# Last MLP as an explicit pipeline with residuals on the tensor engine, score repeats counted ahead of each slot, and a norm's root in four pieces

## The chip, the cores and the metric

The kernel runs on one core of one Trainium2 chip. The metric is the device time of one execution in microseconds (us); medians over several executions are quoted. A "span" is the time from the first to the last instruction of the one execution that was profiled; it is about 2 us shorter than the device time of that execution. The engines: **PE** (TensorE, matmuls), **PEld** (its weight loads), **ACT** (ScalarE, here the exponentials), **DVE** (VectorE), **SP** (SyncE, which only issues transfers here). DVE takes its instructions in the order of the program, so one that waits holds back those behind it: below, DVE stands 7.36 us before one reciprocal, and the copy listed after it runs only then.

## The reference

Two transformer layers on 2048 rows of 512 columns, 32 heads of 16, an MLP of width 1792, all bfloat16; A and B use the same weights in both layers.

```python
x = A_x                                              # (1, 2048, 512)
x = x + A(layernorm(x), A_wqkv, A_wo)                # 32 heads, softmax(q k^T / 4) v, then @ wo
x = x + B(layernorm(x), B_w1, B_w2)                  # relu(x @ w1) @ w2
x = x + A(layernorm(x), A_wqkv, A_wo)                # second layer
return x + B(layernorm(x), B_w1, B_w2)
```

## The kernel before

The loop runs over "slots" of three score blocks (128 keys by 512 queries of one head each). In a slot PE makes scores (32-row tiles), ACT takes their exponential, PE multiplies the exponentials with the values (32-column tiles). Some blocks' exponentials are made on DVE, in chains of several steps; two such blocks are a "pair", and each pair takes work off ACT. All other work (projections, MLP, norms) is kept in queues and fitted into gaps. Three places matter.

**1. Repeated score matmuls.** PE repeats a slot's scores to stay busy; the aim is that its clock isn't lowered:

```python
MM = 216.0                      # ns of one matmul step
FLOOR = 0.56                    # share of a slot in which PE should be busy
...
spare = int(max(need_by - pe_start("s", s_ready), 0.0) / MM)
times = 1 + min(spare, 0 if level >= 0 else 1 if level > -MM else 2)
for _ in range(times):
    ...                         # three score matmuls, the same result each time
...
level = min(level + busy[0] - FLOOR * (exp_end[no] - exp_end[no - 1]), 90.0)
```

**2. The sums of a "segment"** (four heads, 512 queries). `u` holds the unnormalised outputs and the rows of sums. The sums go to 128 partitions in a small transfer (c<-u), are inverted, go back (u<-c) and are broadcast (r<-u, 256 KB); then one DVE multiply makes `ot`. There are two buffers of each, so segment n waits for the multiply of segment n - 2:

```python
if n > 1:
    run_until(("m", n - 2))
u, r, c = ubuf[n % 2], rbuf[n % 2], cbuf[n % 2]
...
nc.sync.dma_start(out=c[:], in_=sums); mark(("c", n), lag=2600.0)   # planner: there after 2.6 us
...
def recip():
    nc.vector.reciprocal(out=c[:], in_=c[:])
    nc.sync.dma_start(out=sums, in_=c[:])
    nc.sync.dma_start(out=r[:], in_=...)            # broadcast of each row to 32 partitions
    mark(("r", n), lag=8500.0)
...
if last:
    task(5000, direct, ots, [("po",)])              # last segment: shuffle, no transfer
else:
    task(250, recip, [("r", n)], [("c", n)])        # at the end of DVE's queue
    task(700, lambda: mul(0, QS), ots + [("m", n)], [("r", n)] + war)
```

`run_until` emits the task at once, whatever it must wait for.

**3. The tail.** After the last slot, `run_all()` emits what is left in the queues, one group of matmuls after the other: output projection, DVE adds x, norm, transposes, all 14 groups of the MLP's first matrix, then the second's.

The softmax here doesn't subtract the row's maximum and nothing guards it: scores larger than these inputs give would overflow.

## Time and profile before

| | before |
|---|---|
| median (4 runs) | 1855.53 us (1851.55 to 1857.51) |
| span of the profiled execution | 1860.6 us |
| end of ACT's last exponential | 1788.4 us |
| tail, from there to the end | 72.2 us |
| ACT idle ahead of exponentials | 28.9 us |

Three more lines of before: the first two are from the groups of instructions (busy us, mean ns of one, idle time of the engine just before them and what ended it); the third is a row of the table of stretches, with the columns that the prediction explains.

```profile
L903 PE MATMUL ps_s<-q,ktp 32*128 32x512 bf16 x6099 | 706.5, 394 | 145.6 <-ACT e L926 127.6 <-DVE ktp L462 1.7 <-DVE x L515 0.6
L664 DVE RECIPROCAL c<-c 128x16 f32<-128x16 f32 x63 | 15.5, 246 | 36.8 <-DMA c<-u 36.8
...
1120.00:1140.00 20.00, 16.00 (x106) 3.42 (x104) 4.26 (x8) 16.07 (x12) 0.00 (x0) 0.67 0.16 33
```

DVE stood for 36.8 us before reciprocals, waiting for the small transfer of the sums. Between 1120 and 1140 us ACT lost 3.93 us at a clock of 0.67.

### The profile page before, as it was taken

To read this page: it belongs to the slowest core of one execution; us is meant where nothing else is said; L and a number is where in the kernel's file an instruction comes from. 1 tells how busy PE (TensorE), PEld (TensorE's weight loads), DVE (VectorE), ACT (ScalarE), POOL (GpSimd) and SP (SyncE) were. 2 spreads that over 40 slices of the span, in tenths; PEclk is the share of its full clock that TensorE was granted. 3 is DMA by queue.
4 is the path that set the end of the run, shared out by engine and by line. 5 is a ranking of instruction groups with operands and counts; after the bars stand their busy time and mean duration, and the time that the engine had idled before them with its cause. 6 is when DMAs were issued, how large, how long until landed. Compare 5 with 4: busy or idle time off the path is not lost.

```text
span 1860.6 us, 28967 instructions
## 1 busy us (share of the span) xinstructions
PE 1660.1 (89%) x12509; PEld 521.9 (28%) x12509; DVE 1170.9 (63%) x1796; ACT 1749.7 (94%) x1380; POOL 2.4 (0%) x35
## 2 busy tenths in 40 slices
PE   8898889999889999899999889989988999889966
PEld 2222222322222232223232221222222222222222
DVE  7446767777766975778332224776767767586662
ACT  6999998999999999999999998999999999999940
POOL 0000000000000000000000000000000000000000
PEclk9999998999999999999899986999999999999988
DMA  4000000210001000110010001011000110001001
GB/s 142 1 13 8 19 13 7 44 22 12 8 21 44 9 11 13 36 25 12 13 29 12 1 19 25 13 33 30 18 16 13 36 30 19 13 19 41 21 9 39
DMA packets 92739, 42.20 MB, mean 23 GB/s; under 512 B 76612, under 2 KB 84548, under 8 KB 92612
## 3 DMA queue, kind: packets, MB, share of 16 engines
q1 hardware_dynamic: 91268, 39.06, 9.3%
q8 instruction: 97, 1.59, 0.4%
q10 hardware_dynamic: 1344, 1.31, 0.2%
q14 instruction: 30, 0.25, 0.0%
HBM read 20.71 MB, written 2.10 MB: 12 GB/s over the span
## 4 chain that ended last, share of the span: by engine, by line
ACT 84%; PE 10%; DVE 3%; DMA 2%; issue 0%; SPq 0%; DVEq 0%
ACT e L926 84%; PE ps_s L903 4%; PE ps_o L696 2%; PE ps_s L360 2%; PE ps_f L360 1%; DMA c<-u 1%; DVE stats L379 0%; DMA r<-u 0%; DMA wqkv<-in_A_wqkv_dram 0%; DVE ht L542 0%; DVE q L497 0%; DVE vaug L490 0%; DVE ot L656 0%; DVE r L678 0%; DMA u<-c 0%
## 5 line engine op out<-in xcount | busy, mean ns | idle before, releaser
L926 ACT ACTIVATE e<-ps_s 128x1536 bf16<-128x1536 f32 (+1 forms) x1366 | 1741.2, 1588 | 28.9 <-PE ps_s L903 27.9
L903 PE MATMUL ps_s<-q,ktp 32*128 32x512 bf16 x6099 | 706.5, 394 | 145.6 <-ACT e L926 127.6
L696 PE MATMUL ps_o<-e,vaug 128*32 128x512 bf16 x3862 | 554.0, 399 | 6.7 <-DVE u L643 3.3
L903 PEld LDWEIGHTS <-ktp 32*128 32x128 bf16 x6099 | 216.7, 93 | 577.6 <-issue 521.2
L696 PEld LDWEIGHTS <-vaug 128*32 128x32 bf16 x4564 | 163.7, 94 | 461.3 <-issue 435.1
L737 DVE TENSOR_SCALAR di<-ps_s 128x512 int32<-128x512 f32 x234 | 160.8, 688 | 101.2 <-PE ps_s L903 99.8
L767 DVE SCALAR_TENSOR_TENSOR de<-dy,di 128x1024 bf16<-128x1024 f32 x117 | 143.1, 1223 | 8.9 <-PE ps_o L696 2.5
L767 DVE SCALAR_TENSOR_TENSOR dy<-dm 128x1024 f32<-128x1024 f32 x117 | 142.9, 1221 | 2.4
L767 DVE SCALAR_TENSOR_TENSOR dy<-dy,dm 128x1024 f32<-128x1024 f32 x117 | 142.8, 1220 | 2.1
L542 DVE TENSOR_SCALAR ht<-ps_f 128x512 bf16<-128x512 f32 x99 | 68.1, 688 | 101.3 <-PE ps_f L360 100.8
L360 PE MATMUL ps_f<-xn2T,w 128*128 128x512 bf16 x400 | 122.5, 383 | 3.4 <-DVE ht L542 0.6
L360 PE MATMUL ps_f<-w,ht 128*128 128x512 bf16 x392 | 123.3, 385 | 0.5
L656 DVE SCALAR_TENSOR_TENSOR ot<-u,mask,r 128x512 bf16<-128x512 f32 (+1 forms) x67 | 48.0, 716 | 82.1 <-DMA r<-u 82.0
L360 PE MATMUL ps_f<-xnT,wqkv 128*128 128x512 bf16 x280 | 88.8, 392 | 4.2 <-DVE vaug L490 1.4
L497 DVE TENSOR_SCALAR q<-ps_f,qmask 128x512 bf16<-128x512 f32 x78 | 55.9, 744 | 48.2 <-PE ps_f L360 48.1
L696 PE MATMUL ps_o<-de,vaug 128*32 128x512 bf16 x468 | 84.2, 387 | 0.0
L761 DVE TENSOR_SCALAR di<-di 128x1024 int32<-128x1024 int32 x117 | 80.8, 691 | 2.9
L761 DVE TENSOR_SCALAR dm<-di 128x1024 int32<-128x1024 int32 x117 | 80.6, 689 | 1.5
L360 PE MATMUL ps_f<-wo,ot 128*128 128x512 bf16 x224 | 71.6, 389 | 0.9 <-DVE x L515 0.4
L696 PE MATMUL ps_o<-di,vaug 128*32 128x512 bf16 x234 | 58.8, 395 | 0.0
L360 PEld LDWEIGHTS <-w 128*128 128x128 bf16 x448 | 36.2, 98 | 73.4 <-issue 59.3
L360 PEld LDWEIGHTS <-ht 128*128 128x128 bf16 x448 | 34.5, 97 | 70.1 <-issue 57.0
(74 smaller groups left out, 496.2 us busy)
## 6 DMA issues: line engine op xcount, KB each, us to landing
r<-u SPq DMA_DIRECT2D x63, 256.0 KB
w<-in_B_w_dram SPq DMA_DIRECT2D x112, 128.0 KB
out_dram<-x SPq DMA_DIRECT2D x16, 128.0 KB
x<-in_A_x_dram SPq DMA_DIRECT2D x14, 128.0 KB
w<-in_B_w_dram SPq DMA_DIRECT2D x1, 1792.0 KB
wqkv<-in_A_wqkv_dram ACTq DMA_DIRECT2D x2, 512.0 KB
c<-u SPq DMA_DIRECT2D x63, 8.0 KB
u<-c SPq DMA_DIRECT2D x63, 8.0 KB
```

Of the source, the lines that this page charges most:

```text
L360: nc.tensor.matmul(b, lhsT, rhs, start=(i == 0), stop=(i == n - 1))
L497: nc.vector.tensor_scalar(out=qbuf[n % 2][e][:], in0=b, scalar1=qmask[e][:, 0:1], scalar2=None, op0=ALU.mult,)
L542: nc.vector.tensor_scalar(out=ht[ft], in0=b, scalar1=0.0, scalar2=None, op0=ALU.max)
L656: nc.vector.scalar_tensor_tensor(out=ot[t][:, a : a + w], in0=u[:, a : a + w], scalar=mask[e][:, 0:1], in1=r[:, a : a + w], op0=ALU.mult, ...
L696: nc.tensor.matmul(ps_o[32 * g : 32 * g + 32, :], vaug[sg["l"]][kb][:, 4 * sg["T"] + g, 2 * e : 2 * e + 32], rhs, start=g not in sg["begun ...
L737: first = nc.vector.tensor_scalar(out=di[:, half, :].bitcast(I32), in0=src, scalar1=EXP_BIAS, scalar2=0.0, op0=ALU.add, op1=ALU.max,)
L761: nc.vector.tensor_scalar(out=out[:].bitcast(I32), in0=di[:].bitcast(I32), scalar1=keep, scalar2=put, op0=ALU.bitwise_and, op1=ALU.bitwise_or,
L767: nc.vector.scalar_tensor_tensor(out=out[:], in0=x[:], scalar=c, in1=y[:], op0=ALU.add, op1=ALU.mult)
L903: nc.tensor.matmul(b[:, w, :], kt[32 * g : 32 * g + 32, kc : kc + P], qbuf[sg["n"] % 2][sg["e"]][32 * g : 32 * g + 32, :], start=True, sto ...
L926: ex = nc.scalar.activation(out=eb[:, :m, :], in_=b[:, :m, :], func=ACTF.Exp, scale=1.0 / (LOG2E * UNIT),)
```

## The change

Its intent: (a) keep PE's clock up by counting the repeats that a slot will need before it runs, instead of paying back a debt one slot late; (b) write out the tail by hand, with h and z matmuls alternating, the residual opened in PSUM by an identity matmul, and copies shared by ACT and DVE; (c) let other DVE work in between the pieces of a norm's root; (d) shorten the start.

```diff
-        times = 1 + min(spare, 0 if level >= 0 else 1 if level > -MM else 2)
+        short = FLOOR * 1330.0 - level - busy[0] - MM * (1 + (len(pend) > 1))
+        times = 1 + min(spare, max(0, math.ceil(short / MM)))
...
-            task(2400, lambda: ln_rstd(tag), [("rs", tag)], all4("st", tag))
+            for part in range(4):
+                task(600, lambda part=part: ln_rstd(tag, part), [("rs", tag, part)], ...)
...
-            task(5000, direct, ots, [("po",)])
+            last_steps.append(direct)
         else:
-            task(250, recip, [("r", n)], [("c", n)])
+            task(250, recip, [("r", n)], [("c", n)], place=0)
...
     run_all()
+    free, lasts = ps_s[1 - slot[0] % 2], ps_s[slot[0] % 2]
+    banks = [free[:, w, :] for w in range(W)] + [ps_f[:]]
+    more = [lasts[:, w, :] for w in range(W)] + [ps_o[:]]
+    for i in rows:
+        add(banks[i], ident[:], x_t[j * TPC + i][:], True, False)      # residual
+        for t in range(NT - 1):
+            add(banks[i], ot[t][:, i * P : (i + 1) * P], wo[:, t // 2, :], False, False)
+    for i in rows:
+        last_steps[0](i)
+        add(banks[i], ot[NT - 1][...], wo[...], False, True)
+        nc.scalar.copy(out=x_t[j * TPC + i][:], in_=banks[i])
+    ...                                             # statistics, root, scales, transposes
+    for ft in range(NF + 1):                        # h(ft), relu on DVE or ACT, then z(ft - 1)
+        ...
```

In this excerpt two assignments are joined into one line and long argument lists are cut ("..."). At the start, the masks go ahead of the first norm and all four scales ahead of the transposes.

More of the change, by code (lines that the diff above doesn't have):

```diff
@@ L380, in ln_stats, with ln_rstd @@
         nc.vector.bn_aggr(out=mv[ln_n(tag)][:, i, :], in_=st[:])
-    def ln_rstd(tag):
+    def ln_rstd(tag, part):
         n = ln_n(tag)
         a, y, t1 = va_[n], ya_[n], ta_[n]
-        nc.vector.tensor_scalar(
-            out=a[:], in0=mv[n][:, :, 1], scalar1=EPS, scalar2=None, op0=ALU.add
-        )
-        nc.vector.tensor_scalar(
-            out=t1[:].bitcast(I32), in0=a[:].bitcast(I32), scalar1=1, scalar2=None,
-            op0=ALU.logical_shift_right,
-        )
-        nc.vector.tensor_scalar(
-            out=y[:].bitcast(I32), in0=t1[:].bitcast(I32), scalar1=-1.0,
-            scalar2=float(RSQRT_SEED), op0=ALU.mult, op1=ALU.add,
-        )
-        for _ in range(3):
-            nc.vector.scalar_tensor_tensor(
-                out=t1[:], in0=y[:], scalar=-0.5, in1=y[:], op0=ALU.mult, op1=ALU.mult
-            )
-            nc.vector.tensor_mul(out=t1[:], in0=t1[:], in1=a[:])
-            nc.vector.scalar_tensor_tensor(
-                out=y[:], in0=t1[:], scalar=1.5, in1=y[:], op0=ALU.add, op1=ALU.mult
-            )
+        if part == 0:
+            nc.vector.tensor_scalar(
+                out=a[:], in0=mv[n][:, :, 1], scalar1=EPS, scalar2=None, op0=ALU.add
+            )
+            nc.vector.tensor_scalar(
+                out=t1[:].bitcast(I32), in0=a[:].bitcast(I32), scalar1=1, scalar2=None,
+                op0=ALU.logical_shift_right,
+            )
+            nc.vector.tensor_scalar(
+                out=y[:].bitcast(I32), in0=t1[:].bitcast(I32), scalar1=-1.0,
+                scalar2=float(RSQRT_SEED), op0=ALU.mult, op1=ALU.add,
+            )
+            return
+        nc.vector.scalar_tensor_tensor(
+            out=t1[:], in0=y[:], scalar=-0.5, in1=y[:], op0=ALU.mult, op1=ALU.mult
+        )
+        nc.vector.tensor_mul(out=t1[:], in0=t1[:], in1=a[:])
+        nc.vector.scalar_tensor_tensor(
+            out=y[:], in0=t1[:], scalar=1.5, in1=y[:], op0=ALU.add, op1=ALU.mult
+        )
     def ln_apply(tag, j, i):
@@ L411, in ln_apply, with ln_transpose @@
         )
-    def ln_transpose(tag, i):
-        pt = bank().bitcast(BF16)
+    def ln_transpose(tag, i, b=None):
+        pt = (bank() if b is None else b).bitcast(BF16)
         for c in range(NDC):
@@ L429, in ln_rows @@
         if i == TPC - 1:
-            task(2400, lambda: ln_rstd(tag), [("rs", tag)], all4("st", tag))
+            for part in range(4):
+                task(
+                    600, lambda part=part: ln_rstd(tag, part), [("rs", tag, part)],
+                    [("rs", tag, part - 1)] if part else all4("st", tag),
+                )
             for k in range(TPC):
@@ L433, in ln_rows @@
                     420, lambda k=k: ln_apply(tag, j, k), [("xn", tag, k)],
-                    [("xT", prev, k), ("rs", tag)],
+                    [("xT", prev, k), ("rs", tag, 3)],
                 )
@@ L538, in fin @@
         def fin(b):
-            if wide[0] and ft % 2:
-                nc.scalar.activation(out=ht[ft], in_=b, func=ACTF.Relu)
-            else:
-                nc.vector.tensor_scalar(
-                    out=ht[ft], in0=b, scalar1=0.0, scalar2=None, op0=ALU.max
-                )
+            nc.vector.tensor_scalar(
+                out=ht[ft], in0=b, scalar1=0.0, scalar2=None, op0=ALU.max
+            )
             mark(("h", l, j, ft))
@@ L623 @@
     norm_no = [0]
+    last_steps = []
     def finish_segment(sg, last):
@@ L673, in recip, with direct @@
             mark(("r", n), lag=8500.0)
-        def direct():
-            nc.vector.stream_shuffle(out=r[:], in_=u[:], mask=[lane] * 32)
-            for a in range(0, QS, P):
-                nc.vector.reciprocal(out=r[:, a : a + P], in_=r[:, a : a + P])
-                mul(a, P)
+        def direct(i):
+            if i == 0:
+                nc.vector.stream_shuffle(out=r[:], in_=u[:], mask=[lane] * 32)
+            a = i * P
+            nc.vector.reciprocal(out=r[:, a : a + P], in_=r[:, a : a + P])
+            mul(a, P)
         ots = [("ot", l, j, t, i) for i in range(TPC)]
         if last:
-            task(5000, direct, ots, [("po",)])
+            last_steps.append(direct)
         else:
-            task(250, recip, [("r", n)], [("c", n)])
+            task(250, recip, [("r", n)], [("c", n)], place=0)
             task(700, lambda: mul(0, QS), ots + [("m", n)], [("r", n)] + war)
-        if t == NT - 1:
+        if t == NT - 1 and not last:
             work.extend(rest_of_chunk(l, j))
@@ L802 @@
     idle_matmuls(18)
-    for i in range(TPC):
-        ln_stats(tag, 0, i)
-    ln_rstd(tag)
-    for i in range(TPC):
-        ln_apply(tag, 0, i)
-        pt = ln_transpose(tag, i)
-        if i % 2:
-            nc.vector.tensor_copy(out=xnT[0][:, :, i * P : (i + 1) * P], in_=pt)
-        else:
-            nc.scalar.copy(out=xnT[0][:, :, i * P : (i + 1) * P], in_=pt)
-        mark(("xnT", tag, i))
-        idle_matmuls(1)
     for e in range(2):
@@ L824 @@
         )
+    for i in range(TPC):
+        ln_stats(tag, 0, i)
+    for part in range(4):
+        ln_rstd(tag, part)
+    for i in range(TPC):
+        ln_apply(tag, 0, i)
+    for i in range(TPC):
+        pt = ln_transpose(tag, i)
+        if i % 2:
+            nc.scalar.copy(out=xnT[0][:, :, i * P : (i + 1) * P], in_=pt)
+        else:
+            nc.vector.tensor_copy(out=xnT[0][:, :, i * P : (i + 1) * P], in_=pt)
+        mark(("xnT", tag, i))
+        idle_matmuls(1)
     for i in range(3):
@@ L965, with add @@
         run_dve(0.0, musts)
-    wide[0] = True
     run_all()
+    l, j = 1, NQS - 1
+    tag = ("ln2", l, j)
+    rows = range(TPC)
+    free = ps_s[1 - slot[0] % 2]
+    lasts = ps_s[slot[0] % 2]
+    banks = [free[:, w, :] for w in range(W)] + [ps_f[:]]
+    more = [lasts[:, w, :] for w in range(W)] + [ps_o[:]]
+    def add(b, lhsT, rhs, first, last):
+        nc.tensor.matmul(b, lhsT, rhs, start=first, stop=last)
+    for i in rows:
+        add(banks[i], ident[:], x_t[j * TPC + i][:], True, False)
+        for t in range(NT - 1):
+            add(banks[i], ot[t][:, i * P : (i + 1) * P], wo[:, t // 2, :], False, False)
@@ new lines @@
+    for i in rows:
+        x = x_t[j * TPC + i]
+        last_steps[0](i)
+        add(banks[i], ot[NT - 1][:, i * P : (i + 1) * P], wo[:, (NT - 1) // 2, :], False, True)
+        nc.scalar.copy(out=x[:], in_=banks[i])
+    for i in rows:
+        ln_stats(tag, j, i)
+    for part in range(4):
+        ln_rstd(tag, part)
+    for i in rows:
+        ln_apply(tag, j, i)
+    for i in rows:
+        pt = ln_transpose(tag, i, more[i])
+        if i % 2:
+            nc.vector.tensor_copy(out=xn2T[:, :, i * P : (i + 1) * P], in_=pt)
+        else:
+            nc.scalar.copy(out=xn2T[:, :, i * P : (i + 1) * P], in_=pt)
@@ new lines @@
+    for i in rows:
+        add(banks[i], ident[:], x_t[j * TPC + i][:], True, False)
+    for ft in range(NF + 1):
+        if ft < NF:
+            n = (l * NQS + j) * NF + ft
+            b = more[ft % 4]
+            for c in range(NDC):
+                add(b, w1buf[n % NW1][:, c, :], xn2T[:, c, :], c == 0, c == NDC - 1)
+            if ft % 2:
+                nc.scalar.activation(out=ht[ft], in_=b, func=ACTF.Relu)
+            else:
+                nc.vector.tensor_scalar(
+                    out=ht[ft], in0=b, scalar1=0.0, scalar2=None, op0=ALU.max
+                )
+            load_w1(n + NW1)
+        if ft:
+            for i in rows:
+                add(
+                    banks[i], ht[ft - 1][:, i * P : (i + 1) * P], w2[:, ft - 1, :],
+                    False, ft == NF,
+                )
@@ L971 @@
+    for i in rows:
+        tt = j * TPC + i
+        if i % 2:
+            nc.vector.tensor_copy(out=x_t[tt][:], in_=banks[i])
+        else:
+            nc.scalar.copy(out=x_t[tt][:], in_=banks[i])
+        nc.sync.dma_start(out=out_flat[tt * P : (tt + 1) * P, :], in_=x_t[tt][:])
 _INS = ['A_x', 'A_wqkv', 'A_wo', 'B_x', 'B_w1', 'B_w2']
```

## The prediction

> **What bounds the kernel now.** I read the page's busy table and its chain of waits first.
>
> ```profile
> PE 1660.1 (89%) x12509; PEld 521.9 (28%) x12509; DVE 1170.9 (63%) x1796; ACT 1749.7 (94%) x1380; POOL 2.4 (0%) x35
> ...
> ACT 84%; PE 10%; DVE 3%; DMA 2%; issue 0%; SPq 0%; DVEq 0%
> ```
>
> ScalarE's exponentials carry 84% of the chain. The group table gives them 1741.2 us in 1366 instructions, and the change does not touch that work. So what can be won is the time in which ScalarE is idle: 1860.6 - 1749.7 = 110.9 us. To see where it lies I took the busy times in stretches of 20 us. The columns are stretch, length, then the busy us (and number of instructions) of PE, weight loads, DVE, ACT, POOL, then granted clock, DMA share, GB/s.
>
> ```profile
> 280.00:300.00 20.00, 19.31 (x142) 5.63 (x141) 13.16 (x20) 20.00 (x16) 0.00 (x0) 1.00 0.07 15
> 300.00:320.00 20.00, 18.57 (x114) 3.99 (x112) 15.96 (x30) 15.31 (x13) 0.00 (x0) 0.60 0.00 0
> ...
> 900.00:920.00 20.00, 18.98 (x113) 3.96 (x110) 1.09 (x3) 16.74 (x13) 0.00 (x0) 0.57 0.07 14
> ...
> 1140.00:1160.00 20.00, 20.00 (x109) 3.95 (x110) 13.53 (x17) 15.70 (x13) 0.00 (x0) 0.50 0.10 21
> ...
> 1800.00:1820.00 20.00, 10.12 (x36) 3.92 (x35) 9.51 (x30) 0.00 (x0) 0.00 (x0) 0.67 0.00 1
> ```
>
> Where the clock is 1.00, ACT is busy 20.00 of 20. Where it falls, TensorE is nearly always busy at half speed and ACT waits for scores. Adding ACT's idle time over the stretches from 120 to 1180 us whose clock is below 1 gives 1.9 (120 to 160), 5.0 (300 to 340), 3.3 (900), 1.8 (1020), 2.7 (1080), 8.9 (1120 to 1180): about 23 us. Some 15 us go before ACT is in stride, and the rest, about 72 us from ACT's last exponential at 1788.4 to the end, is the **tail**, which the chain in order of time shows:
>
> ```profile
> 1784.64 1.78 DMA u<-c
> 1786.44 6.63 DMA r<-u
> 1793.18 0.69 DVE ot L656
> ...
> 1799.61 0.69 DVE x L515
> 1800.35 6.42 PE ps_s L360 x16
> ...
> 1843.03 6.22 PE ps_s L360 x28
> 1849.27 0.70 DVE x L558
> 1850.01 3.20 PE ps_s L360 x14
> 1853.23 0.70 DVE x L558
> 1853.97 3.20 PE ps_s L360 x14
> 1857.19 0.69 DVE x L558
> ```
>
> In it DVE and PE take turns, each waiting for the other; the clock of 0.67 shows the price.
>
> **What the Trainium skill says.** (1) "TensorE: Matmul & The Clock Gate", Part 1, says the array's clock is full or half, and that a busy or an idle window of about 3.4 us switches it. The trace agrees: the same full-size matmul steps by 0.43 us just after 1800.35 and by 0.215 us after 1843. (2) Its Part 3 says that 32-row tiles run concurrently. The trace agrees: three score matmuls take 0.39 us together and PE starts its next kind 0.32 us later, so one repeat of a slot's scores costs 0.22 us of PE, not 0.65. (3) "VectorE: DVE Perf Modes", The DRAIN you can't avoid, says each DVE operation flushes its pipe before the next. I see the cost in the norm's root: twelve operations on 128x4 elements, each near 0.16 us, start 0.20 us apart, 2.4 us in all (1813.38 to 1815.76). (4) "PSUM — Partial Sum Buffer", The four PSUM rules, says a group is started by its first matmul and later ones add to it. So an identity matmul of x can open a group and carry the residual, at one matmul for one DVE addition; the trace of before has no such group to test.
>
> **The change, part by part.**
>
> *Tail.* The last score row's tables: now the reciprocal for the segment before the last runs only at 1784.37 (line 664), 20 us after its sums were copied, behind the queued exponential chain. Its two transfers land at 1793.18 and hold DVE, so the last segment's direct normalisation starts at 1793.86. With the reciprocal put first in the queue, I choose to believe that both transfers land before the loop ends; direct work then starts after the copy of u, at 1788.84 + 0.69 = 1789.55: **4.3 us** won. Its four multiplies end 2.1, 3.3, 4.6 and 5.8 us after its start in the trace, so by 1795.4. PE meanwhile opens four banks with identity and 28 output-projection matmuls, 32 x 0.215 = 6.9 us from 1788.8, to 1795.7, warm; four more finish at 1796.6. ACT copies the four out at 0.6 us each, to 1798.7. Before, the last x was ready at 1810.15 (11.4 us later, the 4.3 included).
> Statistics overlap these copies (0.8 us each): last aggregate 1799.6, root 2.4, so 1802.0. The scales (0.35 pitch), transposes and copies, now alternating engines, end near 1805.0; four cold identity matmuls (4 x 0.43) let the MLP start near 1805.9. Before it started at 1821.70: 15.8 us won so far.
> The MLP has 14 x (4 + 4) = 112 matmuls in both, but h and z now alternate. A relu (0.60 to 0.69 us plus some 0.3 of handover) has 8 matmuls x 0.215 = 1.7 us to hide in, where now h groups wait 0.7 to 0.85 us again and again, and z waits for every h. I count 3 more us cold (7 x 0.43) and 105 x 0.215 = 22.6, so PE ends near 1831.6; the copies on two engines add 1.4, the last store 2.7 as now (1857.88 to 1860.6). End 1835.8: **the tail gives 24.8 us**. The w1 loads: a buffer is wanted again 3 steps, 5.2 us, later; today such a load, issued at 1823.60, was no wait at 1828.09, so I count none.
>
> *Score repeats.* The group table shows 6099 score matmuls for 4096 blocks, 1.49 passes a slot. A slot lasts 1.34 us, one score pass and one value pass 0.43 us: 0.32 of it. The old rule adds passes only after its balance has gone negative, a slot late, and a dip follows every burst of projection work. Ahead of 900 and of 1020 us the trace has one-pass slots with no other matmul, ahead of 1080 slots of two passes (0.48), and the clock then drops. At 1099 to 1105, with 0.56 mean, it stays. The new rule wants 0.56 x 1.33 = 0.745 us less credit in each slot, before it runs: (0.745 - 0.432)/0.216 rounds up to 2 extra passes in an empty slot, three in all, 0.65 busy. Three passes, one value pass and two switches take 1.07 of 1.33 us, so ACT should not wait while warm. I expect score matmuls to rise to about 7000.
>
> *Root in four pieces.* Twelve operations stay twelve; the total is unchanged. Near 301 to 303.5 us they hold back the copy of u, PE waits 1.18 us for it and the clock falls: 5 us of loss. Pieces of 0.6 us let that copy in.
>
> *Start.* The mask work (some 0.6 us) moves into DVE's wait for x; four scales run before the transposes, whose copies finished at 13.11 us. I get 11.5: **1.5 us**.
>
> *What the middle yields.* Of 23 us, the stretch from 1124 (9 us) begins with DVE held 7 us by a sums transfer that queued behind a 256 KB broadcast; nothing in the change shortens that, and while cold, three passes cost more than two. That leaves 14. But the timed median is 8.6 us below the profiled execution (1853.75 against 1862.37), so I take the typical timed run to hold some 14/23 of these losses: 9, and 1 us for a milder stretch at 1124: **10 us**.
>
> Sum: 24.8 + 1.5 + 10 = 36.3; 1853.75 - 36.3 = 1817.4, taken as 1817.
>
> **Rivals.** *The repeats make PE the bound.* PE is 89% busy by the page, and cold slots of nine score matmuls already take 1.94 us against 1.51 with six. For it: every slot comes closer to its limit. Against: warm stretches show ACT at 20.00. If true, the middle gives nothing or loses 5 us: 1827 to 1833. *The earlier reciprocal blocks DVE on its transfer.* DVE is in order and already waited 36.8 us in 10 such cases. For it: it now comes promptly. Against: DVE is 63% busy. A wait of 1 us in every fifth of 63 segments would cost 5 to 12 us if it reached PE. *The clock holds throughout*, also at 1124: 5 us more, 1812. *The tail stays cold*: PE has little to do from 1796.6 to 1802.5, so the MLP could start and stay longer at half speed; each further 3.4 us cold costs 1.7.
>
> **Range and chances.** The tail I trust to 4 us, the middle to 9. Together about 10: 1806 to 1831. Two per cent is 1816.7, almost my figure: faster 0.50, within 0.49, slower 0.01.
>
> **What would show it.** Last exponential to the end: 47 us in place of 72. No wait for r in the tail. The MLP near 26 us, with relus hidden. Clock 1.00 at 300, 900, 1020, 1080 us; a dip near 1124 stays. Score matmuls near 7000. The prediction is wrong if ACT waits for scores at full clock, if DVE waits for c grow, or if the timed runs had lost nothing to the clock: then only 26 us are won, 1827.

## The result, and the profile after

| | before | after |
|---|---|---|
| median | 1855.53 us (1851.55 to 1857.51) | 1837.68 us (1837.21 to 1839.46) |
| profiled span | 1860.6 | 1836.0 |
| ACT idle ahead of exponentials | 28.9 | 23.9 |
| last exponential's end | 1788.4 | 1781.1 |
| tail | 72.2 | 54.9 |

The ratio is 0.9908, 95% interval 0.9888 to 0.9928. Here and below a ratio is the mean time of one kernel's runs over that of the other's of the same rounds, so not quite the ratio of the medians. Executions over 1.5% slower than the fastest of the same kernel are left out of the means.

First the page's busy row and the group of score matmuls, after:

```profile
PE 1688.4 (92%) x13535; PEld 533.9 (29%) x13709; DVE 1172.0 (64%) x1795; ACT 1751.8 (95%) x1388; POOL 2.4 (0%) x35
...
L911 PE MATMUL ps_s<-q,ktp 32*128 32x512 bf16 x7287 | 778.2, 384 | 99.2 <-ACT e L934 77.2 <-issue 2.0 <-DVE ktp L468 1.5
```

There are 1188 more score matmuls, and ACT's busy time is what it was. The stretches, after:

```profile
80.00:100.00 20.00, 17.28 (x105) 5.39 (x103) 5.94 (x11) 14.52 (x11) 0.00 (x0) 0.83 0.00 0
300.00:320.00 20.00, 18.48 (x177) 6.02 (x174) 18.99 (x37) 20.00 (x17) 0.00 (x0) 1.00 0.01 2
900.00:920.00 20.00, 18.38 (x153) 5.78 (x149) 4.48 (x8) 20.00 (x16) 0.00 (x0) 1.00 0.06 14
1100.00:1120.00 20.00, 14.74 (x129) 4.37 (x127) 4.26 (x8) 15.38 (x12) 0.00 (x0) 0.82 0.17 34
1120.00:1140.00 20.00, 19.53 (x114) 3.71 (x109) 6.91 (x11) 14.28 (x12) 0.00 (x0) 0.50 0.16 32
1140.00:1160.00 20.00, 19.27 (x141) 4.62 (x140) 10.80 (x14) 15.62 (x12) 0.00 (x0) 0.65 0.04 8
```

The dips at 300 and 900 us (and those at 1020 and 1080) are gone: ACT is busy 20.00 of 20. How much of this the new repeats did, two profiles can't say; e1 comes back to it. But the **hole** from 1100 to 1160 us is wider: 4.62 + 5.72 + 4.38 = 14.7 us of ACT are lost, 8.9 before. And at 80 to 100 us ACT now loses 5.48 us, 1.70 before. What makes the hole shows in the timeline of after (start, us, engine, line, operation; in brackets the idle time before it and what ended that):

```profile
1106.21 0.52 SPq L652 DMA_DIRECT2D c<-u  x1
...
1112.54 0.25 DVE L668 RECIPROCAL c<-c 128x16 f32<-128x16 f32 x1 [7.36 <-DMA c<-u]
...
1115.33 0.62 PE L701 MATMUL ps_o<-e,vaug 128*32 128x512 bf16 x4 [3.64 <-DVE u L647]
...
1115.88 1.46 PE L911 MATMUL ps_s<-q,ktp 32*128 32x512 bf16 x9
...
1117.39 1.45 ACT L934 ACTIVATE e<-ps_s 128x1536 bf16<-128x1536 f32 x1 [3.89 <-PE ps_s L911]
```

The sums' small transfer, issued at 1106.21, lands 6.3 us later. DVE stands before the reciprocal for 7.36 us. Behind that stands the copy of u, which PE needs before it may write the next values into the accumulator: PE idles 3.64 us, ACT 3.89, and the clock falls. Then nine score matmuls take 1.46 us; at full clock nine took 0.82 (at 1103.75).

The tail, after, from the chain of waits in order of time:

```profile
1775.61 0.16 DVE c L668
1775.80 1.79 DMA u<-c
1777.60 6.65 DMA r<-u
1784.30 0.06 issue
1784.36 0.76 DVE ot L660
...
1792.67 0.59 ACT x L995
1793.27 0.04 issue
1793.31 0.39 PE ps_s L984
1793.72 0.59 ACT x L995
```

Two things cost time here. The reciprocal of the segment before the last still ran only at 1775.6, though its sums had been asked for at 1756.6, so its broadcast still ended after the loop. And a copy out of a bank (ACT) waits for the last matmul of the bank before (PE) and that for the copy before: one bank each 1.05 us.

### The profile page after: what moved, and what is told of

It is laid out like the page before. It is cut to its first block, busy times and chain, and to the rows that moved or that the text cites. A ratio compares the mean times of both kernels' runs of the same rounds, so it can differ in the third digit from the quotient of the medians.

```text
span 1836.0 us, 31204 instructions
## 1 busy us (share of the span) xinstructions
PE 1688.4 (92%) x13535; PEld 533.9 (29%) x13709; DVE 1172.0 (64%) x1795; ACT 1751.8 (95%) x1388; POOL 2.4 (0%) x35
## 4 chain that ended last, share of the span: by engine, by line
ACT 82%; PE 11%; DVE 4%; DMA 2%; issue 1%; SPq 0%; DVEq 0%; ACTq 0%
ACT e L934 82%; PE ps_s L911 4%; PE ps_o L701 3%; PE ps_f L360 2%; PE ps_s L984 1%; DMA c<-u 1%; DVE dy L772 1%; DVE di L742 1%; DVE de L772 0%; DMA r<-u 0%; DVE dm L766 0%; DVE q L503 0%; PE ps_f L984 0%; DVE vaug L496 0%; DVE stats L379 0%
## 5 line engine op out<-in xcount | busy, mean ns | idle before, releaser
L934 ACT ACTIVATE e<-ps_s 128x1536 bf16<-128x1536 f32 (+1 forms) x1366 | 1738.8, 1520 | 23.9 <-PE ps_s L911 23.0
L911 PE MATMUL ps_s<-q,ktp 32*128 32x512 bf16 x7287 | 778.2, 384 | 99.2 <-ACT e L934 77.2
L701 PE MATMUL ps_o<-e,vaug 128*32 128x512 bf16 x3860 | 547.0, 393 | 5.6 <-DVE u L647 4.5
L911 PEld LDWEIGHTS <-ktp 32*128 32x128 bf16 x7287 | 232.7, 92 | 530.9 <-issue 460.8
L360 PE MATMUL ps_f<-xn2T,w 128*128 128x512 bf16 x346 | 114.3, 384 | 5.8 <-issue 1.9
L360 PE MATMUL ps_f<-w,ht 128*128 128x512 bf16 x349 | 110.6, 384 | 4.1 <-issue 3.0
L360 PE MATMUL ps_f<-xnT,wqkv 128*128 128x512 bf16 x235 | 78.0, 389 | 4.4 <-issue 2.3
L360 PE MATMUL ps_f<-wo,ot 128*128 128x512 bf16 x195 | 63.9, 385 | 2.9 <-issue 2.2
L649 DVE COPY u<-ps_o 128x512 f32<-128x512 f32 x48 | 33.1, 690 | 30.2 <-PE ps_o L701 30.1
L468 DVE CAST ktp<-ps_f 128x512 bf16<-128x512 f32 x31 | 21.4, 690 | 44.4 <-PE ps_f L360 38.2
```

Of the source, the lines that this page charges most:

```text
L360: nc.tensor.matmul(b, lhsT, rhs, start=(i == 0), stop=(i == n - 1))
L468: nc.vector.tensor_copy(out=ktp[l][T][j][:], in_=b)
L649: nc.vector.tensor_copy(out=u[:], in_=ps_o[:])
L701: nc.tensor.matmul(ps_o[32 * g : 32 * g + 32, :], vaug[sg["l"]][kb][:, 4 * sg["T"] + g, 2 * e : 2 * e + 32], rhs, start=g not in sg["begun ...
L911: nc.tensor.matmul(b[:, w, :], kt[32 * g : 32 * g + 32, kc : kc + P], qbuf[sg["n"] % 2][sg["e"]][32 * g : 32 * g + 32, :], start=True, sto ...
L934: ex = nc.scalar.activation(out=eb[:, :m, :], in_=b[:, :m, :], func=ACTF.Exp, scale=1.0 / (LOG2E * UNIT),)
```

## The experiments

Two accounts had to be told apart. **Theory**: the tail gave most of what was won, and in the loop the new repeats win their dips but pay it back in the hole. **Rival**: the repeats are worthless or harmful by themselves, because PE becomes the limit. Each run has 3 rounds against before, and four executions of its own. The groups e1 to e4, e5 to e8 and e9 to e12 ran on three different chips, so a difference of 1 or 2 us between kernels of different groups is not sure. The kernel before had a median of 1855.51 us in the rounds of e1 to e4, 1853.76 in those of e5 to e8, and 1853.53 in those of e9 to e12, each on 7 runs. All twelve kernels gave correct results.

### e1: the tail alone

Before, with the new tail only (old repeats, root whole, old start, old place of the reciprocal).

```diff
 # kernel before
+    last_steps = []
-            task(5000, direct, ots, [("po",)])
+            last_steps.append(direct)
-    wide[0] = True
     run_all()
+    ...   # the tail of the change, with one ln_rstd(tag)
```

> The kernel before with the explicit last MLP alone (old repeat rule, root in one piece, old start, reciprocal at the end of the queue). Theory A (the tail gave nearly all of the gain, the new repeats next to nothing net): last exponential to the end 54 to 56 us instead of 72, time 1837 to 1841 us, ratio about 0.991. Theory B (repeats and the other parts carry a third or more): 1844 to 1848 us.

Measured: 1840.07 us (1838.63 to 1841.33), ratio 0.9917 (0.989 to 0.9945); tail 55.8 us. The tail alone gives 15.4 us, most of the 17.9 of the whole change.

Up to its end, the loop of e1 is that of before, instruction for instruction. Yet in its profiled execution (clock 0.979, before 0.966) ACT loses nothing at 120 to 160 and at 900 us and 0.40 us at 300, where in that of before it lost 1.9, 3.3 and 5.0; over the loop it loses 21.3 us in place of 28.9. The dip at 1020 and the hole are there in both:

```profile
900.00:920.00 20.00, 17.61 (x138) 5.49 (x138) 4.48 (x8) 20.00 (x16) 0.00 (x0) 1.00 0.06 14
1020.00:1040.00 20.00, 19.16 (x132) 6.06 (x131) 6.47 (x11) 17.94 (x14) 0.00 (x0) 0.88 0.00 1
1120.00:1140.00 20.00, 19.78 (x112) 3.75 (x111) 4.82 (x10) 15.00 (x11) 0.00 (x0) 0.51 0.16 32
```

So dips of several us come and go between executions of one loop, and a dip that is missing in one profile is not yet the work of an edit.

### e2: the repeats alone

```diff
 # kernel before
-        times = 1 + min(spare, 0 if level >= 0 else 1 if level > -MM else 2)
+        short = FLOOR * 1330.0 - level - busy[0] - MM * (1 + (len(pend) > 1))
+        times = 1 + min(spare, max(0, math.ceil(short / MM)))
```

> The kernel before with the new repeat rule alone. Theory A (the rule removes five clock drops, but opens one near 90 us and lengthens the one near 1100 us): within 4 us of before, 1851 to 1857 us; clock 1.00 at 900, 1020 and 1080 us; ACT loses 5 us near 90 us and 14 instead of 9 us between 1100 and 1165 us. If the drop near 300 us stays, the root in four pieces was what removed it. Theory B (the rule is worth the 10 us that the prediction gave it): 1844 to 1847 us.

Measured: 1854.38 us (1852.85 to 1856.79), ratio 0.9996 (0.9968 to 1.0024): nothing. The stretches say why:

```profile
900.00:920.00 20.00, 18.38 (x159) 5.89 (x156) 4.45 (x8) 20.00 (x16) 0.00 (x0) 1.00 0.07 14
...
1120.00:1140.00 20.00, 20.00 (x116) 3.82 (x116) 5.89 (x11) 14.43 (x11) 0.00 (x0) 0.50 0.16 33
```

There is no dip at 900 us (e1 has none either, so this row alone doesn't show the rule at work), and none at 1000 to 1100 us, where e1 loses 5.2. But 1100 to 1180 us loses 14.7 us of ACT, where e1 with the old rule loses 9.1: PE is busy 20.00 of 20 at half speed, and its score groups are longer.

### e3: the whole change with the old repeats

```diff
 # changed kernel
-        short = FLOOR * 1330.0 - level - busy[0] - MM * (1 + (len(pend) > 1))
-        times = 1 + min(spare, max(0, math.ceil(short / MM)))
+        times = 1 + min(spare, 0 if level >= 0 else 1 if level > -MM else 2)
```

> The changed kernel with the old repeat rule put back. Theory A: 1835 to 1841 us, so no more than 3 us from the changed kernel; ACT loses about 9 us between 1100 and 1165 us rather than 14.7, and 2 us near 90 us rather than 5.5, while drops of 2 to 4 us each are back where ScalarE has no projection work beside it. Theory B (the new rule helps): 1845 us or more.

Measured: 1840.59 us (1837.28 to 1845.41), ratio 0.9922 (0.9891 to 0.9954): 2.9 us above the change, within its own spread.

```profile
900.00:920.00 20.00, 19.87 (x118) 4.02 (x112) 2.32 (x4) 16.91 (x13) 0.00 (x0) 0.60 0.06 14
...
1120.00:1140.00 20.00, 17.52 (x116) 3.97 (x116) 4.27 (x8) 16.84 (x12) 0.00 (x0) 0.67 0.16 33
```

The same exchange from the other side: the dips of 3.1 (900), 1.6 (1020) and 3.3 us (1060 to 1100) are back, 8.0 in all; the hole loses 9.5 us in place of 14.7, and the stretch from 80 to 100 us 3.14 in place of 5.48. Summed over the loop, ACT loses 25.9 against 23.9. By this pair of profiles the repeats win about 8 us and give some 7.5 back, 5.2 in the hole and 2.3 at 80 to 100 us. The profiled execution of e3 was the slowest of its four (1845.41 us), so 8 us is the upper end.

### e4: the small transfer on a queue of its own

Why does the small transfer land 6 us late? If it queues behind the broadcast on SP's queue, another queue frees it.

```diff
 # changed kernel
-                nc.sync.dma_start(out=c[:], in_=sums)
+                nc.gpsimd.dma_start(out=c[:], in_=sums)
```

> The changed kernel with the small read of the sums issued from GpSimd's queue, so that it does not stand behind the 256 KB broadcast on the sync queue. Theory A (the drop at 1100 to 1165 us is DVE, in order, held up to 7 us by that read): its waits for the sums fall from 37 us in total to under 15, the clock stays 1.00 there, ACT loses under 3 us in place of 14.7, time 1823 to 1828 us. Theory B (the clock falls there for lack of array work, whatever DVE does): no change beyond 2 us, 1836 to 1839 us.

Measured: 1838.71 us (1832.34 to 1840.85), ratio 0.9903 (0.9864 to 0.9941): no gain. The edit did not shorten the waits as it was meant to, so it doesn't decide between its two theories: DVE still waits 34.2 us in 10 cases, the hole loses 14.9 us, and a transfer issued at 1098.66 lands at about 1105.5, together with the broadcast. This agrees with the Trainium skill, "DMA: Bandwidth & Descriptors", Issuing engines are not separate DMA queues: transfers of any issuing engine interleave on the same 16 engines.

### e5: the reciprocal really first

`place=0` puts the reciprocal at the head of DVE's queue, but each step of an exponential chain is then inserted at the position equal to the number of chain steps queued, which is ahead of it. This edit makes the planner prefer it whenever its sums are due.

```diff
 # changed kernel
-                        can.append((2, ready, t))
+                        can.append((0.5 if "first" in t else 2, ready, t))
...
             task(250, recip, [("r", n)], [("c", n)], place=0)
+            maker[("r", n)]["first"] = True
```

> The changed kernel with the reciprocal of the sums really ahead of the exponential chain in DVE's queue (its place at the front does not hold: a chain that begins while the sums are under way is inserted ahead of it). Theory A (this is the term of the tail that failed): the direct normalisation starts within 1 us of the copy of u, DVE waits for no broadcast in the tail, the array is not left idle there; last exponential to the end 50 to 52 us in place of 54.9, time 1832 to 1836 us. Theory B (the tail is long for other reasons): tail within 1 us of 54.9, time 1836 to 1839 us.

Measured: 1839.78 us (1837.61 to 1840.36), ratio 0.9912 (0.9885 to 0.9939). The tail is 51.4 us, 3.5 shorter: the reciprocal runs at 1766.7 and the last segment starts right after its copy. But the loop ends 6 us later (1787.15), and the median is above the ranges of both theories. Two rows show what else moved, first of the changed kernel, then of e5 (last step of a pair's chain):

```profile
L772 DVE SCALAR_TENSOR_TENSOR de<-dy,di 128x1024 bf16<-128x1024 f32 x118 | 144.3, 1223 | 9.1 <-PE ps_o L701 2.4 <-PE ps_s L911 0.5
```

```profile
L773 DVE SCALAR_TENSOR_TENSOR de<-dy,di 128x1024 bf16<-128x1024 f32 x110 | 134.5, 1223 | 8.1 <-PE ps_o L702 2.3 <-PE ps_s L912 0.5
```

With reciprocals ahead of chains, the planner started 8 pairs fewer on DVE, and ACT made those blocks: its exponentials take 1744.9 us instead of 1738.8. So the mechanism in the tail is right, and its gain is paid for on the bottleneck.

### e6: e5, with the banks of one PSUM tile kept apart

Three banks belong to one tile, and the dependency tracking orders engines by tile. The edit declares that accesses to different banks need no order.

```diff
 # e5, tail only
+    def apart(engine, made_by, key):
+        tile_key, bank_key = key
+        for other, on, ins in touched.setdefault(tile_key, []):
+            if other != bank_key and on != engine:
+                tc.declare_no_dep(made_by.ins, ins, reason="another bank of the same tile")
+        touched[tile_key].append((bank_key, engine, made_by.ins))
```

> As the run with the sums first, and the last MLP's instructions on different banks of one PSUM tile no longer wait for each other. Theory A (the shared tile, not the engines, puts the four copies of x 1.05 us apart instead of 0.6, and the transposes 1.2 us): 2 to 3 us less than the run with the sums first. Theory B (the waits are hidden by DVE's statistics): under 0.7 us less.

Measured: 1835.68 us (1835.11 to 1837.18), ratio 0.9893 (0.9866 to 0.992); tail 46.9 us. That is 4.1 us below e5, where 2 to 3 were expected. In the chain the copies no longer take turns with PE; the statistics follow each other at 0.8 us:

```profile
1794.06 0.59 ACT x L1013
...
1794.67 0.71 DVE stats L379
...
1795.58 0.59 DVE stats L379
```

The results stayed correct. The Trainium skill, "PSUM — Partial Sum Buffer", PSUM bank collisions raise a hardware error, says that two engines in different banks run clean; this run agrees.

### e7: the whole change with four buffers for the sums

Two edits of one purpose: DVE should not be sent to wait for sums that can't be there. Four buffers put the forced multiply two segments later, and for the segments that add stored sums in the second layer the planner expects the transfer after 7.5 us rather than 2.6.

```diff
 # changed kernel; r and c likewise
-    ubuf = [sb([P, QS], FP32, f"u{n}") for n in range(2)]
+    ubuf = [sb([P, QS], FP32, f"u{n}") for n in range(4)]
...
-        if n > 1:
-            run_until(("m", n - 2))
+        if n > 3:
+            run_until(("m", n - 4))
...
-                mark(("c", n), lag=2600.0)
+                mark(("c", n), lag=7500.0 if sg["load"] is not None and l == 1 else 2600.0)
```

> The changed kernel with four buffers for the sums and their broadcast in place of two, and the reciprocal of the second layer's short segments queued 7.5 us after the copy in place of 2.6, so that DVE need not stand before a transfer. Theory A (the drop from 1100 to 1165 us is DVE, in order, held by transfers of 6 to 7 us in segments of 7 us): DVE waits for the sums in that stretch fall under 3 us, ACT loses under 4 us there in place of 14.7, time 1825 to 1829 us. Theory B (the clock drops there whatever DVE does, or the transfers only move the wait to the broadcast): over 10 us lost there, 1835 to 1839 us.

Measured: **1819.45 us** (1816.45 to 1819.81), ratio 0.98 (0.9767 to 0.9832), clock 0.995; theory A had expected no less than 1825. The row of DVE's reciprocals, and the stretch of the hole:

```profile
L668 DVE RECIPROCAL c<-c 128x16 f32<-128x16 f32 x63 | 15.4, 245 | 1.6 <-DMA c<-u 1.5
...
1120.00:1140.00 20.00, 17.73 (x175) 5.89 (x176) 16.20 (x22) 20.00 (x17) 0.00 (x0) 1.00 0.15 30
```

The waits for sums fall from 37.2 to 1.5 us, and ACT is busy 20.00 of 20 through the whole hole. ACT's loss over the loop falls from 23.9 to 9.0 us, and the time by 18.2. So the hole is made by DVE standing before late sums, with the copy of u behind them. Waiting as such is not it: between 1090 and 1180 us DVE now stands 19.3 us before the broadcast (r<-u), 7.9 in the changed kernel, and PE and ACT lose nothing to it. Which of the two edits takes the hole away was not separated.

### e8: the old repeats until the first layer's projections are made

```diff
 # changed kernel
+        if any(key not in made for key in first_layer):
+            times = 1 + min(spare, 0 if level >= 0 else 1 if level > -MM else 2)
+        else:
+            short = ...; times = ...            # the new rule
```

> The changed kernel with the old repeat rule until the first layer's keys are all projected, then the new one. Theory A (repeats took array time from the first layer's projections, which are then made in one forced burst at 90 us): ACT loses at most 3.2 us between 80 and 100 us in place of 5.5, clock 1.00 there, time 1834 to 1836 us. Theory B (the burst comes from the root in pieces or the new start): unchanged at 5 us or more.

Measured: 1839.35 us (1836.91 to 1841.32), ratio 0.9911 (0.9883 to 0.9939): no change in time. ACT's loss at 80 to 100 us falls from 5.48 to 3.50 us, with the clock back at 1.00, and 1 us comes on at 40 to 60. In e1, which has neither the new rule nor the new start, that stretch loses 1.34; in e2, with the new rule alone, 3.14; in e3, with all but the new rule, also 3.14. So the new rule is about half of what the change added there; which other part of the change is the rest, was not found.

### e9: four buffers and the old repeats

What are the repeats worth once the hole is gone?

```diff
 # e7
-        short = ...; times = ...                # the new rule
+        times = 1 + min(spare, 0 if level >= 0 else 1 if level > -MM else 2)
```

> Whole change with the sums buffers four deep and the later wait (as in e7), but with the old repeat rule. Theory A (the new repeats are worth the 8 us of the dips at 900, 1020 and 1080 us, and this was only hidden by the longer hole at 1100 that they caused; with the hole gone their worth shows): the dips of 3.1, 1.6 and 3.3 us come back, the hole stays away, the time is 8 us above e7, near 1827. Rival B (the repeats are worth nothing once the sums no longer stall DVE, since the same relief moves the bursts ahead of the dips): within 3 us of e7, 1817 to 1822, and no dip of over 2 us at 900 to 1100.

Measured: 1832.51 us median, but the four runs were 1851.19, 1837.13, 1827.33 and 1827.88, ratio 0.9903 (0.9847 to 0.9958). The profiled one is the first, and its clock was 0.85 in stretches where PE never stopped, so it doesn't place the dips. The two runs with a clock of 0.987 lie 8 us above e7 (clock 0.995), as the theory said, and no run is as fast as any of e7. I take that as support for the theory, not as a measurement of 8 us: it picks two of four runs, and e7 ran on another chip.

### e10: four buffers on the kernel before

The edit of e7 on before.

> Kernel before with only the sums buffers four deep and the later wait. Theory A (the hole at 1100 to 1180 us is made by those waits in either kernel): the 8.9 us of the hole go, the dips at 300, 900, 1020 and 1080 stay, the time is 9 us below before, near 1846. Rival B (the hole moves to another place where two sums transfers meet the broadcast): within 3 us of before.

Measured: 1846.63 us (1843.48 to 1850.39), ratio 0.9968 (0.9947 to 0.9988), 6.9 us below before. ACT is busy 20.00 of 20 in all of 1100 to 1180 us, with the old repeats and the old tail. The hole belongs to the sums in both kernels. The other dips did not stay as expected: 900 us lost nothing, 300 us 0.40, 1020 to 1100 us still 4.9, all as in e1.

This settles what the repeats do at 900 to 1100 us. In the four profiles with the old rule and a clock that reaches 1.00 (before, e1, e3, e10) ACT loses 7.7, 5.2, 8.1 and 5.2 us there; in the eight with the new rule (the change, e2, e4 to e8, e12) at most 0.4. So the new rule does remove these dips, and they are worth 5 to 8 us.

### e11: e7 with the banks kept apart

The edit of e6 on e7, without that of e5.

> e7 and in its tail no order kept between different banks of one PSUM tile. Theory A (copies out and transposes wait for each other only through the shared tile): the four copies of x come 0.65 us apart rather than 1.05, the tail is 2 to 4 us shorter, 1816 to 1817. Rival B (the array is then idle longer and turns cold, which takes the gain back): within 1 us of e7.

Measured: **1816.08 us** median; three runs lie at 1815.93 to 1816.19. The fourth, the profiled one, took 2359.89 us at a mean clock of 0.556; it is left out. Ratio 0.9796 (0.9779 to 0.9812). By the medians that is 3.4 us below e7, at the strong end of what was expected; but e7 ran on another chip, one of its runs took 1816.45 us, and by the ratios to before only 0.7 us lie between them. So the gain over e7 is likely (e6 shows the mechanism, and gained 4.1 us over e5 on one chip) but not measured here. It is the lowest median, and beats both kernels.

### e12: e11 and the reciprocal really first

> e11 and the reciprocal really first in the queue. Theory A (in e5 the reciprocal first cost 8 blocks made by VectorE, which is 6.6 us of ScalarE, because VectorE stood waiting for late sums; with deeper buffers the sums are there, so the count stays near 118 and the tail gains its 3.4 us): near 1813. Rival B (moving the reciprocals ahead shifts the exponential chains whatever the transfers do): pairs near 110 and the time 2 to 4 us above e11.

Measured: 1819.83 us (1819.56 to 1821.41), ratio 0.9818 (0.9803 to 0.9833), 3.8 us **above** e11. There are 110 pairs again, and ACT's exponentials take 1742.4 us against 1736.5 in e7. DVE's waits for sums are only 3.4 us here, so waiting is not what costs the pairs: moving the reciprocals ahead of the chains does. The rival was right, and my reason for the 8 lost pairs in e5 was wrong.

## Why the prediction was right or wrong

The prediction was 1817 us with a range of 1806 to 1831; the time is 1837.68 us, outside it. It gave 0.50 to a gain of over 2% and 0.49 to less; 0.9908 is less. Most of its mechanisms hold. Its two large terms, the tail and the middle, were mis-sized, the start gave nothing that shows, and one loss was not foreseen.

**"the tail gives 24.8 us"**: it gave 72.2 - 54.9 = 17.3. Two assumptions of that sum failed.
- "With the reciprocal put first in the queue, I choose to believe that both transfers land before the loop ends." They did not. The broadcast landed 3.3 us after the last exponential, and the direct normalisation began at about 1785.0, 3.9 us after it, where I had 1.15: 2.7 us lost. I had read `place=0` and not what the later insertions do to it. e5 mended this: 1.2 us.
- "ACT copies the four out at 0.6 us each": they came 1.05 us apart, since each waited for PE through the shared tile, as did the transposes; PE was idle and then cold. The MLP, predicted 17.5 us after the last exponential, began 24.0 after it (1805.15 - 1781.1), 2.7 of these 6.5 us from the transfers. The last copies and the store cost another us.
- With both mended (e6) the tail is 46.9 us, where I had 47.4. The rest of the sum is right to within 2 us, partly by luck: in e6 the MLP begins 18.1 us after the last exponential (17.5 predicted) and takes 24.1 us (25.7 predicted). In the change itself it took 1830.8 - 1805.15 = 25.7 us, with relus hidden and no wait for w1. The rival "the tail stays cold" does not hold in the MLP, only ahead of it. The identity matmul as the start of a PSUM group, which I took from the Trainium skill, "PSUM — Partial Sum Buffer", The four PSUM rules, gives correct results.

**"What the middle yields": 10 us.** Alone, the repeats gave 1.1 us (e2), within the noise. The dips at 900, 1020 and 1080 us that I named did go, for 5 to 8 us (see e10), and the score matmuls are 7287 where I said about 7000. What failed is the last term, "1 us for a milder stretch at 1124". I had seen that DVE stands before the sums there, and that "while cold, three passes cost more than two", and still counted a gain. It became a loss of 5.8 us (14.7 against 8.9). This was a weighed risk with the wrong sign: the rule that keeps PE warm in a thin slot lengthens every slot once it is cold. Where the hole is taken away (e7), the dips stay away too, and their 5 to 8 us remain won; e9 measures the time loosely. The rival "the repeats make PE the bound" fits only the cold stretches; warm ones with up to three passes have ACT at 20.00.

**"Pieces of 0.6 us let that copy in"** and 5 us at 300: that dip is gone, but it is nearly gone (0.40 us) in e1 and e10 too, whose root is whole. It varies with things that have nothing to do with the root. The pieces are not shown to be worth anything.

**"Start: 1.5 us."** The copies that I put at 11.5 us end at 13.47 (13.11 before), and the first exponential starts at 18.48 (18.22 before): nothing came earlier. Then 20 to 60 us lose 1.6 in place of 3.2, but 80 to 100 us loses 3.8 more. I had not looked at what the new rule does while PE is overfull with the first projections. I had also written that ACT is busy 20.00 of 20 where the clock is 1.00; from 20 to 100 us of before it lost 5.2 us at that clock.

**The earlier reciprocal blocks DVE on its transfer**: the waits for c are 37.2 us, 36.8 before, so this rival did not happen in the change. In e5, where the reciprocal is really first, they are 39.0; the cost came another way, by 8 pairs.

**The clock of the timed runs.** I scaled the losses of the profiled execution by 14/23 for a typical run. The timed runs of before had clocks of 0.964 to 0.980, the profiled one 0.966, so its profile was indeed among the cold ones, and e1 showed the same loop losing 7.6 us less; the tail and repeats measured singly (15.4 + 1.1) add to 16.5 of the 17.9 measured.

In sum, 17.9 us were won in place of 36.3: by the timed runs the tail alone gave 15.4 (e1) where 24.8 were promised, and the loop and the start 2.5 (17.9 - 15.4) where 11.5 were promised. What remains open is the rest of the loss at 80 to 100 us, and why the dips at 300 and 900 us come and go between executions of one loop.

## What to carry to other kernels

A rule that adds filler work to keep the clock up must know whether the clock is up: in a cold stretch the same filler takes nearly twice the time (1.46 us against 0.82), and can cancel all that it wins elsewhere. Before tuning the symptom, find what stalls an in-order engine first: here two more buffers and a later planned arrival were worth as much as the whole change (18.2 us against 17.9), and did away with the larger of the two places where the filler lost again what it had won. And a priority in a scheduler is worth checking in the trace, by the time at which the instruction ran: `place=0` was not first, and once it was, it took work from VectorE that ScalarE had to do.

## What the Trainium skill lacked or had wrong

- "TensorE: Matmul & The Clock Gate", Part 1, says that the array's clock is either full or half, and beside these tells of 13/16 once three cores of a die run dense matmuls, and of a stuck 1/4. This kernel runs on one core (whether others of the die were busy is not on record), and one execution of e9 held 0.85 and the slow one of e11 0.56, evenly for stretches of many us; why, no run shows. In e9 the eight matmuls of an MLP step take 1.99 us (0.25 each, where 0.215 is full), and in e11 3.07 us (0.38 each, where half speed is 0.43). A row of e9's stretches, 2 us long:

```profile
1000.00:1002.00 2.00, 1.97 (x16) 0.64 (x15) 0.34 (x1) 2.00 (x3) 0.00 (x0) 0.85 0.00 0
```

- The same part says that one busy window of about 3.4 us brings the full clock back. It does not say how matmuls on 32-row or 32-column tiles count as busy. In before, PE was busy 14.00 of 14 us with the clock at 0.50 throughout, mostly with such tiles; whether the tiles are why, was not tested:

```profile
1146.00:1160.00 14.00, 14.00 (x84) 2.79 (x80) 11.41 (x13) 11.13 (x9) 0.00 (x0) 0.50 0.09 20
```

- "DMA: Bandwidth & Descriptors", Anatomy of one DMA, gives about 2.0 us fixed plus the bytes over 436 GB/s, fitted on GpSimd's path. The 8 KB transfer u<-c took 1.79 us on SyncE's path, near that. But I found no page that gives the time of a broadcast within SBUF, or of a small transfer beside it: the 256 KB broadcast took 6.65 us, where the fit would estimate 2.6, and the 8 KB c<-u issued during one landed after 6.3 us. While the broadcast ran alone with it (1107 to 1112 us of the change), the mean busy share of the 16 DMA engines was 0.23 to 0.25, what four busy ones would give; why, was not tested.
